# Memory-token attention with a gated MLP, forward and backward: stores on another queue, a normalisation emitted later, eleven head groups

## The chip, the cores and the metric

One core of one Trainium2 chip runs the whole program. The metric is the device time of one execution in microseconds (us); smaller is better. The engines are TensorE (PE in the profile, its weight loads PEld), VectorE (DVE), ScalarE (ACT), GpSimd (POOL) and SyncE (SP, which here only issues DMAs). Each engine works through its own list of instructions in order; semaphores hold an instruction back until what it needs is there, and whatever stands behind it on the same engine waits too.

## The reference

A block with conditioning (six modulation rows from `c`), an attention branch A, a gated MLP branch B, and the gradients of all inputs. What matters is branch A, which is a recurrence:

```python
for s in range(n_seg):                       # 64 segments of 32 rows
    xs = x[:, s * seg_len:(s + 1) * seg_len, :].copy()
    h = jnp.concatenate([mem, xs], axis=1)   # 8 memory rows + 32 rows = 40
    q, k, v = h @ Wq, h @ Wk, h @ Wv         # 32 heads of 128
    p = softmax(where(mask, q k^T * scale, -1e9))
    o = (p v) @ Wo
    mem = o[:, :M, :].copy()                 # the next segment's memory
    outs.append(o[:, M:, :])
```

Segment s cannot start before the first eight output rows of segment s-1 are there. The backward pass runs the same chain from the last segment to the first. (The lines for q, k, v, p and o are shortened.)

## The kernel before

**Phases.** `phase2` is the forward recurrence with the first layer norm in it, `phase3` the MLP forward and backward, `phase4` the backward recurrence, `phase5` the weight gradients of A (large matrix products over rows that phases 2 and 4 left in DRAM). A scheduler orders the instructions of each engine from the program's text and its own estimate of when each becomes ready, so the order on an engine is not that of the source.

**Layout.** 32 heads times 40 rows are kept as groups of three heads: one group holds 3 x 40 = 120 rows in a block of 128 columns. 32 heads need 11 groups (the last holds two). The tiles are built for `G = 12` groups, `G * 128 = 1536` columns, so that three parts (`pi` = 0, 1, 2) of `PG = 4` groups fit the PSUM banks; in phase 2 the twelfth group is skipped by `min(PG, 11 - pi * PG)`, in phase 4 it is computed like the others. Every tile of that layout that goes through DRAM (`OT`, `PS`, `OSR` from phase 2; `DVR`, `DKR`, `DQR` from phase 4) is 128 x 1536 bf16, 384 KB.

**Phase 2, one segment.** `hT` holds the segment's 32 rows: 8 of memory and 24 of x. Its last 8 rows do not depend on the memory; they are projected ahead for four segments at once (`proj_b`, rows `RBv`, `RBk`, `RBq`, turned by `turn_b` into `b_cols`). Position in such a group of four is `s4` (0 to 3); below a *tile* is four segments. For each segment:

- `proj` and `turn` make q, k, v (`RAq`, `RAk`, `RAv`, then `qT`, `kT`, `vT`). The 8 extra columns per head are copied from `b_cols` by GpSimd (L65, four small copies for each of v, k, q).
- The rows of k and q go to DRAM for the backward pass by `rows_out`: two DMAs each on SP (`KST`, `QST`, L455 and L457), and once per tile six DMAs each for the `RB` rows (L461, L464).
- `st_exp` computes the scores and their exponential `ET`, `den` the denominators `rden`, `pv` the output rows `Ost`, `ott` turns them into `OT` (evacuated by ACT, L61), `outproj` multiplies by Wo into `at_ps` (L208).
- `fold_split` cuts `at_ps` into a bf16 head and its remainder (`at_hi` by ACT, L230, `at_lo` by DVE, L231, each in two halves of one tile), `fold_sum` adds the four column blocks (`at_ft`, L239), and ACT copies the memory rows into the next `hT` (L630). That copy ends the segment's part in the recurrence.
- `P` for the backward pass is `ET` transposed by a DMA on SP (`Pst<-ET`, L617; `Pst` has one buffer) and multiplied by `rden` on GpSimd (L635). GpSimd issues the stores of `PS`, `OT`, `OSR` (L637 to L639) and of `VT` (L594).
- `TailRows` collects the last 8 rows of each segment's `OT` on GpSimd (`collect`, L1463, tile `ao_tail`), and after four segments multiplies them by Wo in four pieces (`chunk`, `ao_tps`, L208); their fold goes through `self.later`. `fill(s4, ...)` puts the next tile's `proj_b` and `turn_b` at named places of the segment.

**Phase 4, one segment** (backwards): `OT`, `Pst`, `VT`, `Qst`, `Kst` are loaded on SP; `dot_bank` (`proj_ps`, L1124), `dost`, `ds_part` (L1142, L1146), `grad_part` (L1155) and `dstt` work in parts of four groups; each of dV, dK, dQ is transposed by a DMA on SP (`rows_x`, L1160) and stored by GpSimd (L1161); `dht` sums into `dh_ps`, which is folded as in phase 2 and gives the next segment's `dyT` (L1216).

Of the kernel before, what the change touches and what calls it, by code (L numbers as in the profile page):

```python
# [19 lines left out]
class Cfg:  # L20
    def __init__(self, NS=64, phases=("p0", "p1", "p2", "p3", "p4", "p5")):
        self.S_full = 2048
        self.D = 512
        self.DC = 4
        self.H = 32
        self.E = 128
        self.T = 32
        self.M = 8
        self.L = 40
        self.F = 1792  # L30
        self.FC = 14
        self.NS = NS
        self.S = NS * self.T
        self.NT = self.S // 128
        self.G = 12
        self.XW = 33 * 40 + 8
        self.scale = self.E ** -0.5
        self.phases = phases


class K:
# [181 lines left out]
    def fold_split(self, pool, ps, name):  # L223

        nc = self.nc
        hi = pool.tile([128, 512], BF16, name=name + "_hi", tag="hi")
        lo = pool.tile([128, 512], BF16, name=name + "_lo", tag="lo")
        for h in range(2):
            sl = slice(256 * h, 256 * h + 256)
            nc.scalar.activation(hi[:, sl], ps[:, sl], AF.Copy)  # L230
            nc.vector.tensor_tensor(lo[:, sl], ps[:, sl], hi[:, sl], op=ALU.subtract)  # L231
        return hi, lo

    def fold_sum(self, psp, parts, name, tag):

        ft = psp.tile([128, self.cfg.DC, 32], F32, name=name + "_ft", tag=tag)
        for c in range(self.cfg.DC):
            for i, t in enumerate(parts):
                self.nc.tensor.matmul(ft[:, c, :], lhsT=t[:, c * 128:(c + 1) * 128], rhs=self.foldsel[:],  # L239
                                      start=(i == 0), stop=(i == 1))  # L240
        return ft
# [89 lines left out]
    def phase2(self):  # L331
# [4 lines left out]
        PG = G // NP  # L336
        PW = PG * GW
        with ExitStack() as ctx:
# [74 lines left out]
            def part3(t, pi):  # L413
                return t[:, pi * PW:(pi + 1) * PW].rearrange("p (g x) -> p g x", x=GW)
# [55 lines left out]
            def b_pieces(t):  # L470
# [17 lines left out]
                return {(0, "end1"): [P("k", 0)], (1, "end1"): [P("k", 1)], (2, "end1"): [P("q", 0)], (2, "mid"): [T_("k")],  # L488
                        (2, "end2"): [P("q", 1)], (3, "mid"): [P("v", 0), T_("q")], (3, "end1"): [P("v", 1)], (4, "start"): [T_("v")]}
# [9 lines left out]

            tail = TailRows(self, sb2, psp, psb, 1, "ao", self.AOB)  # L500
            for s in range(NS):
# [24 lines left out]
                def st_exp(pi):  # L526
                    st_ps = ps_f32("st_ps")
                    for j in range(min(PG, 11 - pi * PG)):
# [4 lines left out]
                    n = min(PG, 11 - pi * PG)  # L533
# [4 lines left out]
                def den(pi):  # L538
                    if pi == 0:
                        den_ps[0] = psp.tile([128, G], F32, name="dc_ps", tag="p")  # L540
                    n = min(PG, 11 - pi * PG)
# [6 lines left out]
                def transposes_part(src, pi, w=GW):  # L548
                    ps = ps_b16("tps")
                    n = min(PG, 11 - pi * PG)  # L550
# [9 lines left out]
                def pv(pi):  # L560
                    or_ps = ps_f32("or_ps")
                    n = min(PG, 11 - pi * PG)
# [31 lines left out]
                nc.gpsimd.dma_start(self.VT[s], VT[:, :])  # L594
# [3 lines left out]
                proj("q", 1, "dve")  # L598
                st_exp(0)
# [18 lines left out]
                pv(2)  # L618
                ott(1)
                outproj(0)  # L620
# [6 lines left out]
                self.pop_later()  # L627
# [5 lines left out]
                if s4 == nseg_t - 1:  # L633
                    tail.begin(s - nseg_t + 1, [Wo])
                nc.gpsimd.tensor_tensor(Pst[0:120, 0:11, :], Pst[0:120, 0:11, :],  # L635
                                        rden[:, 0:11].unsqueeze(2).to_broadcast([120, 11, 128]), op=ALU.mult)
                nc.gpsimd.dma_start(self.PS[s], Pst[:])  # L637
                nc.gpsimd.dma_start(self.OT[s], gl3(OT))
                nc.gpsimd.dma_start(self.OSR[s], gl3(Ost))  # L639
# [370 lines left out]
    def phase4(self):  # L1010
# [7 lines left out]
        with self.p4_ctx as ctx:  # L1018
# [10 lines left out]
            PG = G // NP  # L1029
# [24 lines left out]
            def part3(t, pi):  # L1054
                return t[:, pi * PW:(pi + 1) * PW].rearrange("p (g x) -> p g x", x=GW)
# [29 lines left out]
            def transposes_part(src, pi):  # L1085
                ps = ps_b16("tps")
                for j in range(PG):
                    g = pi * PG + j
                    nc.tensor.transpose(ps[:, j, :], src[:, g * GW:(g + 1) * GW], self.ident[:, :])  # L1089
                return ps  # L1090
# [13 lines left out]
            for s in reversed(range(NS)):  # L1104
# [12 lines left out]
                def dot_bank(hb, eng):  # L1117
# [13 lines left out]
                    nc.vector.tensor_tensor(prodO[:, hb * PW:(hb + 1) * PW], dOT[:, hb * PW:(hb + 1) * PW],  # L1131
                                            OT[:, hb * PW:(hb + 1) * PW], op=ALU.mult)

                def dost(pi):
                    ps = transposes_part(dOT, pi)
                    nc.vector.tensor_copy(part3(dOst, pi), ps[:, :, :])

                def ds_part(pi):
                    ps = ps_f32("dp_ps")
                    for j in range(PG):  # L1140
                        g = pi * PG + j
                        nc.tensor.matmul(ps[:, j, :], lhsT=dOT[:, g * GW:(g + 1) * GW], rhs=VT[:, min(g, 10) * 120:min(g, 10) * 120 + GW],  # L1142
                                         start=(j == 0), stop=False, skip_group_check=True)
                    for j in range(PG):
# [3 lines left out]
                    nc.vector.scalar_tensor_tensor(out=part3(dS, pi), in0=ps[:, :, :], scalar=cfg.scale, in1=part3(Pst, pi),  # L1148
                                                   op0=ALU.mult, op1=ALU.mult)

                def grad_part(nm, lh, rh, xt, pi, eng):
                    ps = ps_f32("g_ps")
                    for j in range(PG):
# [3 lines left out]
                    self.evac(eng, part3(xt, pi), ps[:, :, :])  # L1157
# [5 lines left out]
                def dstt(pi):  # L1163
                    ps = transposes_part(dS, pi)
                    nc.vector.tensor_copy(part3(dST, pi), ps[:, :, :])
# [421 lines left out]
```

## Time and profile before

| what | us |
|---|---|
| median of 3 runs | 3884.27 (3883.76 to 3904.68) |
| the profiled execution, its own time | 3890.29 |
| its span from first to last instruction | 3888.5 |
| TensorE busy | 3348.9 (86% of the span) |
| VectorE / ScalarE / GpSimd busy | 1686.8 / 1238.8 / 1102.1 |
| phase 2, first to last `hT` copy | 120.2 to 1391.1 |
| phase 4, first to last `dyT` copy | 2070.6 to 3216.2 |

Busy shares are means over phases with different limits, so each phase is read by itself below. A row of a timeline gives the start, the duration, the engine (SPq is SP's queue), line, operation, out<-in, shapes and count, and in brackets how long the engine had been idle and what released it. A row of waits gives the engine and line that waited, what it waited for, the total, the number of times, and the longest.

### The profile page before, as it was taken

The page shows a single profiled execution, that of the slowest core. Times are in us where ns is not written, and L with a number is a line of the kernel's source. Part 1 is how long each engine was busy: PE and PEld are TensorE (multiplying, and loading weights), DVE is VectorE, ACT ScalarE, POOL GpSimd, SP SyncE. Part 2 cuts the span into 40 slices and gives each one's busy share as a digit, 9 for nine tenths or more (in the row PEclk, how much of TensorE's full clock was granted, in tenths as well). Part 3 has the DMA queues.
Part 4 walks back from the last instruction along what each step waited for, and adds up shares of the span by engine and source line. Part 5 has one row for each costly group of instructions (what it writes and reads, how often), then busy time and mean ns, then how long its engine had stood idle before and what let it go on. Part 6 is the DMA issues. An engine that isn't in the chain of part 4 may idle for free.

```text
span 3888.5 us, 108424 instructions
## 1 busy us (share of the span) xinstructions
PE 3348.9 (86%) x45938; PEld 1940.7 (50%) x46014; DVE 1686.8 (43%) x4087; ACT 1238.8 (32%) x2742; POOL 1102.1 (28%) x2173
## 2 busy tenths in 40 slices
PE   2888888888888869997998989998899994999996
PEld 1444444444444435554545666666566662445453
DVE  2544444444444437764134444544455451322222
ACT  0444444444444435453122322333233331100001
POOL 3444444434433423332112111121112110322221
PEclk6999999999999979999999999999999997999998
DMA  7566655565655663333779999999999999878874
GB/s 227 127 130 134 138 137 130 132 130 137 133 121 125 125 171 121 120 118 106 238 220 232 229 233 219 229 241 224 209 234 244 231 235 194 213 194 200 196 204 144
DMA packets 825642, 692.39 MB, mean 178 GB/s; under 512 B 543850, under 2 KB 716666, under 8 KB 825028
## 3 DMA queue, kind: packets, MB, share of 16 engines
q1 hardware_dynamic: 714852, 422.99, 51.6%
q0 software_dynamic: 51504, 206.62, 15.8%
q10 hardware_dynamic: 58800, 55.84, 5.7%
q8 instruction: 360, 5.90, 0.7%
q14 instruction: 126, 1.03, 0.1%
HBM read 297.01 MB, written 287.61 MB: 150 GB/s over the span
## 4 chain that ended last, share of the span: by engine, by line
PE 55%; DMA 10%; issue 5%; DVE 4%; ACT 2%; POOL 1%; SPq 0%; DVEq 0%; ACTq 0%; POOLq 0%
PE gps L1356 11%; PE dh_ps L208 10%; PE proj_ps L1124 5%; PE g_ps L1155 4%; DMA Pst<-ET 4%; PE gps5o L1366 3%; PE gps L928 3%; PE pass_ps L431 2%; PE mm L842 2%; PE tps L1089 2%; PE dh_tps L208 1%; PE dp_ps L1146 1%; PE dp_ps L1142 1%; PE mm L775 1%; PE mm L779 1%
## 5 line engine op out<-in xcount | busy, mean ns | idle before, releaser
L1356 PE MATMUL gps<-rows,hrows 128*128 128x512 bf16 (+2 forms) x2124 | 415.2, 355 | 1.9
L1356 PEld LDWEIGHTS <-hrows 128*128 128x128 bf16 x2160 | 211.4, 98 | 204.1
L1124 PE MATMUL proj_ps<-dyT,WoT 128*128 128x40 bf16 x8192 | 232.7, 180 | 36.8 <-issue 29.2
L1124 PEld LDWEIGHTS <-WoT 128*128 128x128 bf16 x8192 | 223.3, 96 | 49.8 <-issue 49.8
L635 POOL TENSOR_TENSOR Pst<-Pst,rden 120x1408 bf16<-120x1408 bf16 x64 | 163.2, 2550 | 259.5 <-DMA Pst<-ET 242.1
L431 PEld LDWEIGHTS <-hT 128*32 128x32 bf16 x6144 | 146.4, 99 | 160.9 <-issue 21.0
L63 DVE CAST ot<-gps 128x512 bf16<-128x512 f32 (+3 forms) x77 | 48.9, 635 | 390.9 <-PE gps L1356 206.2
L208 PE MATMUL at_ps<-Wo,OT 128*32 128x512 bf16 x2048 | 169.7, 430 | 49.0 <-ACT OT L61 48.8
L231 DVE TENSOR_TENSOR dh_lo<-dh_ps,dh_hi 128x256 bf16<-128x256 f32 x128 | 54.4, 425 | 333.0 <-ACT dh_hi L230 332.9
L1366 PE MATMUL gps5o<-dyrows,rows 128*128 128x512 bf16 x627 | 139.9, 382 | 45.8 <-DMA rows<-OSR 44.9
L61 ACT ACTIVATE dVT<-g_ps 128x512 bf16<-128x512 f32 x192 | 114.6, 597 | 202.9 <-PE g_ps L1155 156.5
L61 ACT ACTIVATE ot<-gps 128x512 bf16<-128x512 f32 (+3 forms) x77 | 42.5, 552 | 415.4 <-PE gps L1356 239.3
L61 ACT ACTIVATE OT<-tps 128x512 bf16<-128x512 bf16 (+1 forms) x192 | 107.9, 563 | 180.8 <-DMA OT<-OT 79.5
L1360 POOL DMA_DIRECT2D out_dram<-ot x108 | 81.6, 755 | 279.3 <-DVE ot L63 152.0
L63 DVE CAST dKT<-g_ps 128x512 bf16<-128x512 f32 x192 | 131.9, 687 | 63.3 <-PE g_ps L1155 58.8
L208 PE MATMUL dh_ps<-WvT,dVT 128*32 128x512 bf16 x2048 | 153.5, 396 | 3.8 <-issue 3.8
L61 ACT ACTIVATE dOT<-proj_ps 128x480 bf16<-128x480 f32 (+2 forms) x192 | 68.5, 391 | 275.1 <-PE proj_ps L1124 193.5
L231 DVE TENSOR_TENSOR at_lo<-at_ps,at_hi 128x256 bf16<-128x256 f32 x128 | 54.1, 422 | 234.0 <-ACT at_hi L230 231.5
L431 PE MATMUL pass_ps<-Wv,hT 128*32 128x512 bf16 x2048 | 143.1, 422 | 9.5 <-ACT hT L630 9.5
L61 ACT ACTIVATE dQT<-g_ps 128x512 bf16<-128x512 f32 x192 | 114.7, 597 | 112.1 <-PE g_ps L1155 112.1
L63 DVE CAST RAq<-pass_ps 128x512 bf16<-128x512 f32 x128 | 88.5, 692 | 131.4 <-PE pass_ps L431 129.9
L567 DVE TENSOR_TENSOR Ost<-or_ps,rden 120x512 bf16<-120x512 f32 (+1 forms) x192 | 123.6, 644 | 34.4 <-PE dc_ps L544 18.9
(368 smaller groups left out, 7487.5 us busy)
## 6 DMA issues: line engine op xcount, KB each, us to landing
OSR<-Ost POOLq DMA_DIRECT2D x64, 384.0 KB, 4.4
OT<-OT POOLq DMA_DIRECT2D x64, 384.0 KB, 3.3
PS<-Pst POOLq DMA_DIRECT2D x64, 384.0 KB, 4.7
OT_l<-OT SPq DMA_DIRECT2D x64, 384.0 KB
Pst_l<-PS SPq DMA_DIRECT2D x64, 384.0 KB
DVR<-rows_x POOLq DMA_DIRECT2D x64, 384.0 KB, 4.7
DKR<-rows_x POOLq DMA_DIRECT2D x64, 384.0 KB, 6.8
DQR<-rows_x POOLq DMA_DIRECT2D x64, 384.0 KB, 4.3
```

Source lines behind the costliest of these rows:

```text
L61: return nc.scalar.activation(out, in_, AF.Copy)
L63: return nc.vector.tensor_copy(out, in_)
L208: self.nc.tensor.matmul(ps[32 * j:32 * j + 32, :], lhsT=lhsT, rhs=w, start=(n < 4), stop=(n >= total - 4), tile_position=(0, 32 * j))
L231: nc.vector.tensor_tensor(lo[:, sl], ps[:, sl], hi[:, sl], op=ALU.subtract)
L431: nc.tensor.matmul(ps[32 * j:32 * j + 32, :], lhsT=lhs(c), rhs=rhs, start=(c == 0), stop=(c == DC - 1), tile_position=(0, 32 * j))
L567: nc.vector.tensor_tensor(part3(Ost, pi)[0:120, 0:n, :], or_ps[0:120, 0:n, :], rden[:, pi * PG:pi * PG + n].unsqueeze(2).to_broadcast([120 ...
L635: nc.gpsimd.tensor_tensor(Pst[0:120, 0:11, :], Pst[0:120, 0:11, :], rden[:, 0:11].unsqueeze(2).to_broadcast([120, 11, 128]), op=ALU.mult)
L928: nc.tensor.matmul(ps[:], lhsT=h2r[:, j, c * 128:(c + 1) * 128], rhs=xr[:, j, :], start=(j == 0), stop=(j == NT - 1))
L1124: nc.tensor.matmul(ps[:, g_, hl * L:(hl + 1) * L], lhsT=WoT[:, c, h * E:(h + 1) * E], rhs=dyT[:, c, :], start=(c == 0), stop=(c == DC - 1))
L1155: nc.tensor.matmul(ps[:, j, :], lhsT=lh[:, g * GW:(g + 1) * GW], rhs=rh[:, g * GW:(g + 1) * GW], start=True, stop=True)
L1356: nc.tensor.matmul(ps[:, 0:ng * E], lhsT=hrows[:, tp_, c * 128:(c + 1) * 128], rhs=rows[:, tp_, 0:ng * E], start=(tp_ == 0), stop=(tp_ == ...
L1366: nc.tensor.matmul(ps[:], lhsT=rows[:, tp_, gg * E:(gg + 1) * E], rhs=dyrows[:, tp_, :], start=(tp_ == 0), stop=(tp_ == NTP - 1))
```

## The change

Five things change together.

- `G` is 11: all tiles, DRAM tensors, stores, loads and transposes of that layout have 1408 columns (352 KB); in phase 4 the twelfth group is no longer computed. Parts keep four groups (`PG = 4`), the third has three.
- The stores of `VT`, `OT`, `OSR`, `PS` are issued by SP.
- The multiplication of `Pst` by `rden` and the `PS` store are emitted in the next segment, after its `proj`.
- `fold_split` uses four tiles of 256 columns; both `hi` halves come ahead of both `lo` halves.
- In phase 2 the order within a segment and the places of the `proj_b` and `turn_b` pieces differ.

```diff
-        self.G = 12
+        self.G = 11
...
-        hi = pool.tile([128, 512], BF16, name=name + "_hi", tag="hi")
-        lo = pool.tile([128, 512], BF16, name=name + "_lo", tag="lo")
+        parts = []
         for h in range(2):
             sl = slice(256 * h, 256 * h + 256)
-            nc.scalar.activation(hi[:, sl], ps[:, sl], AF.Copy)
-            nc.vector.tensor_tensor(lo[:, sl], ps[:, sl], hi[:, sl], op=ALU.subtract)
-        return hi, lo
+            hi = pool.tile([128, 256], BF16, name=name + "_hi", tag=f"hi{h}")
+            nc.scalar.activation(hi[:], ps[:, sl], AF.Copy)
+            parts.append(hi)
+        for h in range(2):
+            lo = pool.tile([128, 256], BF16, name=name + "_lo", tag=f"lo{h}")
+            nc.vector.tensor_tensor(lo[:], ps[:, 256 * h:256 * h + 256], parts[h][:], op=ALU.subtract)
+            parts.append(lo)
+        return parts
...
-                return {(0, "end1"): [P("k", 0)], (1, "end1"): [P("k", 1)], (2, "end1"): [P("q", 0)], (2, "mid"): [T_("k")],
-                        (2, "end2"): [P("q", 1)], (3, "mid"): [P("v", 0), T_("q")], (3, "end1"): [P("v", 1)], (4, "start"): [T_("v")]}
+                return {(0, "end1"): [P("v", 0)], (1, "end1"): [P("v", 1)], (1, "end2"): [P("k", 0)], (2, "mid"): [T_("v")],
+                        (2, "end1"): [P("k", 1)], (2, "end2"): [P("q", 0)], (3, "end1"): [P("q", 1)], (3, "end2"): [T_("k")],
+                        (4, "start"): [T_("q")]}
...
-                nc.gpsimd.dma_start(self.VT[s], VT[:, :])
+                nc.sync.dma_start(self.VT[s], VT[:, :])
...
+                if norms:
+                    norms.pop()()
                 st_exp(0)
...
                 self.pop_later()
+                vst(2)
                 den(0)
                 pv(0)
-                vst(2)
                 st_exp(1)
                 st_exp(2)
-                ott(0)
+                fill(s4, "mid")
                 den(1)
                 pv(1)
-                tail.chunk()
-                fill(s4, "mid")
+                ott(0)
+                self.pop_later()
                 den(2)
...
                 pv(2)
+                outproj(0)
                 ott(1)
-                outproj(0)
                 ott(2)
...
                 fill(s4, "end1")
-                self.pop_later()
+                tail.chunk()
                 ft = self.fold_sum(psp, parts, "at", "p")
...
-                nc.gpsimd.tensor_tensor(Pst[0:120, 0:11, :], Pst[0:120, 0:11, :],
-                                        rden[:, 0:11].unsqueeze(2).to_broadcast([120, 11, 128]), op=ALU.mult)
-                nc.gpsimd.dma_start(self.PS[s], Pst[:])
-                nc.gpsimd.dma_start(self.OT[s], gl3(OT))
-                nc.gpsimd.dma_start(self.OSR[s], gl3(Ost))
+                nc.sync.dma_start(self.OSR[s], gl3(Ost))
+                nc.sync.dma_start(self.OT[s], gl3(OT))
+
+                def norm(s=s, Pst=Pst, rden=rden):
+                    nc.gpsimd.tensor_tensor(Pst[0:120, :, :], Pst[0:120, :, :],
+                                            rden[:, :].unsqueeze(2).to_broadcast([120, G, 128]), op=ALU.mult)
+                    nc.sync.dma_start(self.PS[s], Pst[:])
+
+                norms.append(norm)
...
             def transposes_part(src, pi):
                 ps = ps_b16("tps")
-                for j in range(PG):
+                n = min(PG, G - pi * PG)
+                for j in range(n):
```

The same replacement of `range(PG)` by `range(n)` is made in `ds_part`, `grad_part` and `dstt` of phase 4.

Where this puts the instructions is seen at three places. The first is TensorE at the end of the last segment of a tile in the middle of phase 2 (`s4 = 3`), before; repeated rows are left out. `at_ft` is the fold that the recurrence waits for, `ao_tail` the collected tail rows of this tile, `p1tp` the first layer norm's transposes for a later tile.

```order
L239 LDWEIGHTS at_hi
L239 MATMUL at_ft<-foldsel,at_hi 128x32
L314 LDWEIGHTS h_14878
L314 MATMUL p1tp<-ident,h_14878 128x128
L208 LDWEIGHTS ao_tail_13656
L208 MATMUL ao_tps<-Wo,ao_tail_13656 32x512
```

With the change the first rows of the same kind stand in the next segment, between its scores (`st_ps`, with the mask) and its second denominators (`dc_ps`).

```order
L538 MATMUL st_ps<-maskT_491,ident 128x120
L208 LDWEIGHTS ao_tail_13727
L208 MATMUL ao_tps<-Wo,ao_tail_13727 32x512
L550 LDWEIGHTS ET_518
L550 MATMUL dc_ps<-ones,ET_518 128x1
L571 LDWEIGHTS ET_518
L571 MATMUL or_ps<-Vst_520,ET_518 128x128
```

Nine of the tail's matmuls thus stood ahead of the last three of the fold that ends the segment; now the first of them comes behind most of the next segment's scores.

The second place is GpSimd around the multiplication of `Pst` at that tile boundary, before.

```order
L65 COPY qT_512<-b_colsq 128x24x8
L635 TENSOR_TENSOR Pst<-Pst,rden 120x1408
L639 DMA OSR<-Ost_522 128x1536
L1463 COPY ao_tail_13656<-OT_524 128x33x8
L637 DMA PS<-Pst 128x1536
L638 DMA OT<-OT_524 128x1536
L318 COPY hb<-hx 128x128
```

And with the change:

```order
L647 TENSOR_TENSOR Pst<-Pst,rden 120x1408
L1479 COPY ao_tail_13727<-OT_524 128x33x8
L65 COPY kT_514<-b_colsk 128x3x8
L322 COPY hb<-hx 128x128
L65 COPY kT_514<-b_colsk 128x24x8
L65 COPY kT_514<-b_colsk 128x3x8
L65 COPY kT_514<-b_colsk 128x2x8
L65 COPY qT_512<-b_colsq 128x3x8
L65 COPY qT_512<-b_colsq 128x24x8
```

The multiplication still stands ahead of the collection of its own segment's tail rows. The three stores are gone from this engine, and at this boundary the k and q copies of the next segment stand behind the multiplication; at the other three boundaries of a tile they stand ahead of it, before and with the change.

The third place is SP between two transposes, before (`H1ROWS` once per tile).

```order
L617 DMA_TRANSPOSE Pst<-ET_518 128x12x128
L311 DMA H1ROWS<-h_18022 128x512
L455 DMA KST<-RAk_528 3x32x1024
L457 DMA KST<-RAk_528 32x3x384
L455 DMA QST<-RAq_530 3x32x1024
L457 DMA QST<-RAq_530 32x3x384
```

And with the change, at the same boundary:

```order
L625 DMA_TRANSPOSE Pst<-ET_518 128x11x128
L643 DMA OSR<-Ost_522 128x1408
L644 DMA OT<-OT_524 128x1408
L649 DMA PS<-Pst 128x1408
L465 DMA QST<-RBq_536 4x8x1024 x3
L468 DMA QST<-RBq_536 4x8x384 x2
L315 DMA H1ROWS<-h_18117 128x512
L600 DMA VT<-vT_516 128x1328
L459 DMA KST<-RAk_528 3x32x1024
L461 DMA KST<-RAk_528 32x3x384
L459 DMA QST<-RAq_530 3x32x1024
L461 DMA QST<-RAq_530 32x3x384
```

`OSR` and `OT` follow the transpose directly; the `PS` store, which waits for the multiplication, stands ahead of the `RB` rows and of the next segment's `VT`, `KST` and `QST`.

More of the change, by code (lines that the diff above doesn't have):

```diff
@@ L527, in st_exp @@
                     st_ps = ps_f32("st_ps")
-                    for j in range(min(PG, 11 - pi * PG)):
+                    for j in range(min(PG, G - pi * PG)):
                         g = pi * PG + j
@@ L1152, in grad_part @@
                     ps = ps_f32("g_ps")
-                    for j in range(PG):
+                    n = min(PG, G - pi * PG)
+                    for j in range(n):
                         g = pi * PG + j
```

45 lines of the change are left out of this document (24 added, 21 removed).

## The prediction

> **What bounds the kernel now.** I read the page's slices first, then the ends of the segments and the stretches of the two recurrences, then the waits of TensorE in each, and last the timeline around the longest waits.
>
> ```profile
> PE   2888888888888869997998989998899994999996
> L630 ACT ACTIVATE hT<-at_ft x63: 197/198/198, 120.2 to 1391.1; 128x32 bf16<-128x32 f32 x63
> L1216 ACT ACTIVATE dyT<-dh_ft x63: 197/198/198, 2070.6 to 3216.2; 128x32 bf16<-128x32 f32 x63
> 120.00:1391.00 1271.00, 1083.16 (x16515) 583.10 (x16513) 583.88 (x1751) 556.37 (x1433) 512.22 (x1257) 0.94 0.59 131
> 2070.00:3216.00 1146.00, 1056.94 (x21206) 715.35 (x21205) 567.74 (x1297) 356.13 (x772) 217.33 (x448) 0.97 1.03 230
> ```
>
> TensorE is the busiest engine everywhere, but the phases differ in what interrupts it. The copy that ends a segment runs 63 times in 1270.9 us in phase 2, 20.5 us a segment (62 intervals), and in 1145.6 us in phase 4, 18.5 us. The last two numbers of the stretches are the DMA share and GB/s: transfers are at 0.59 in phase 2 and at 1.03 in phase 4. The change touches only these two phases, so I price them apart.
>
> **Phase 2: the waits that the change aims at.** The waits of TensorE there, one of ScalarE below them:
>
> ```profile
> PE ao_tps L208 <- POOL ao_tail L1463: 69.8, 15, 8.5
> PE at_ps L208 <- ACT OT L61: 43.7, 14, 4.9
> PE tps L553 <- ACT OT L61: 12.2, 4, 4.4
> ACT at_hi L230 <- DVE at_lo L231: 26.3, 62, 0.5
> ```
>
> The first comes 15 times, once per tile. Its place is the end of an `s4 = 3` segment:
>
> ```profile
> 821.29 4.00 SPq L617 DMA_TRANSPOSE Pst<-ET  x1
> 829.01 2.53 POOL L635 TENSOR_TENSOR Pst<-Pst,rden 120x1408 bf16<-120x1408 bf16 x1 [8.88 <-DMA Pst<-ET]
> 832.07 0.42 POOL L1463 COPY ao_tail<-OT 128x264 bf16<-128x264 bf16 x1
> 832.54 1.46 PE L208 MATMUL ao_tps<-Wo,ao_tail 128*32 128x512 bf16 x9 [8.53 <-POOL ao_tail L1463]
> 834.23 0.20 ACT L630 ACTIVATE hT<-at_ft 128x32 bf16<-128x32 f32 x1 [9.59 <-PE at_ft L239]
> ```
>
> The transpose takes 7.7 us from issue to the start of the multiplication; GpSimd stands at that multiplication, the tail's collection stands behind it, and TensorE stands at the tail's matmuls with the rest of the segment's own fold behind them. In the changed order those matmuls come behind most of the next segment's scores, whose first exponential starts 7.6 us into a segment further down (945.74 less the end of the copy, 938.16); the collection still stands behind the multiplication, but that much earlier than it is needed. I take all **69.8 us**.
>
> The second and third have one cause, seen in an `s4 = 2` segment:
>
> ```profile
> 877.94 2.54 POOL L635 TENSOR_TENSOR Pst<-Pst,rden 120x1408 bf16<-120x1408 bf16 x1 [1.50 <-DMA Pst<-ET]
> 880.42 0.58 POOL L638 DMA_DIRECT2D OT<-OT  x1
> 881.53 0.54 POOL L594 DMA_DIRECT2D VT<-vT  x1
> 886.32 0.60 ACT L61 ACTIVATE OT<-tps 128x512 bf16<-128x512 bf16 x1 [5.47 <-DMA OT<-OT]
> ```
>
> The last segment's `OT` store is issued behind the multiplication, lands late, and ScalarE may not overwrite `OT`. With the change SP issues it right behind the transpose, ahead of anything that waits for the multiplication. What cover it has is seen in a segment without long waits:
>
> ```profile
> 937.96 0.20 ACT L630 ACTIVATE hT<-at_ft 128x32 bf16<-128x32 f32 x1 [0.30 <-PE at_ft L239]
> 945.74 0.57 ACT L534 ACTIVATE ET<-st_ps 128x480 bf16<-128x480 f32 x1 [0.60 <-ACT qT L61]
> 948.85 0.60 ACT L61 ACTIVATE OT<-tps 128x512 bf16<-128x512 bf16 x1 [0.28 <-issue]
> 954.04 0.76 POOL L65 COPY kT<-b_colsk 128x192 bf16<-128x192 bf16 x4
> ```
>
> (The last row, copies for the next segment, is used further down.) `OT` is rewritten 10.7 us after the copy that began the segment; the transpose before it had landed by the multiplication at 941.15 (its row is below), 3.0 us into it. That leaves 7.7 us for a store of 352 KB whose predecessor took 5.9 (880.42 to 886.32). I take 43.7 + 12.2 = **55.9 us**.
>
> Separate halves in the fold remove ScalarE's wait for the first `at_lo`, 26.3 us in 62 times. TensorE has the `proj_b` matmuls to do in some of that time; bounds 0 and 26, I take half, **13 us**. Together 139 us, and the remaining TensorE time of a tile is 4 x 20.5 - 139/16 = 73.3 us.
>
> **Phase 2: what comes in its place.** SP now carries a chain through every segment: multiplication, `PS` store, `VT` store, k and q rows, transpose, next multiplication. Its pieces, from two segments before:
>
> ```profile
> 901.12 0.71 SPq L455 DMA_DIRECT2D KST<-RAk  x1
> 905.18 3.23 SPq L617 DMA_TRANSPOSE Pst<-ET  x1
> 912.47 2.86 POOL L635 TENSOR_TENSOR Pst<-Pst,rden 120x1408 bf16<-120x1408 bf16 x1 [4.39 <-DVE ao_b_tb L247]
> ...
> 927.32 0.72 SPq L455 DMA_DIRECT2D KST<-RAk  x1
> 931.41 4.23 SPq L617 DMA_TRANSPOSE Pst<-ET  x1
> 941.15 2.54 POOL L635 TENSOR_TENSOR Pst<-Pst,rden 120x1408 bf16<-120x1408 bf16 x1 [5.49 <-DMA Pst<-ET]
> ...
> 872.82 2.42 SPq L461 DMA_DIRECT2D KST<-RBk  x3
> 875.28 1.21 SPq L464 DMA_DIRECT2D KST<-RBk  x2
> ```
>
> From the first k row store to the multiplication are 11.4 us and 13.8 us. The multiplication adds 2.54, the issues of `PS` and `VT` 0.54 each (the row of `VT` above): 15.0 to 17.4 us for a plain segment, under TensorE's 73.3 / 4 = 18.3. In two of four segments five or six `RB` stores now stand between `PS` and `VT`: five cost 2.42 + 1.21 = 3.6 us, six about 4.3. The four segments of a tile then make 4 x 15.0 + 0.6 + 4.3 + 3.6 = 68.5 us at the lower length and 78.1 at the upper, against 73.3. The lower adds nothing; the upper adds 4.8 us a tile, 77 us in all. Both are near; I take 2.3 us a tile, **37 us**. The trace cannot show this chain on one queue, so both ends stay in the range. GpSimd loses four issues of about 0.55 us a segment, which it had spare.
>
> [...]
>
> **Phase 4.** Per segment eight movements of a 384 KB tile (two loads, three transposes, three stores) shrink by 32 KB each.
>
> ```profile
> DMA packets 396215, 263.95 MB, mean 230 GB/s; under 512 B 344328, under 2 KB 344328, under 8 KB 396012
> q1 hardware_dynamic: 378697, 185.25, 81.2%
> q0 software_dynamic: 17315, 75.67, 20.4%
> q8 instruction: 166, 2.72, 1.0%
> PE proj_ps L1124 <- issue: 29.2, 10, 5.7
> PE g_ps L1155 <- issue: 13.5, 9, 2.6
> PE tps L1089 <- issue: 11.1, 6, 3.9
> ACT dh_hi L230 <- DVE dh_lo L231: 30.2, 62, 0.5
> 2504.29 0.39 PE L1142 MATMUL dp_ps<-VT_l,dOT 128*128 128x128 bf16 x4
> 2505.64 0.39 PE L1155 MATMUL g_ps<-dS,Qst 128*128 128x128 bf16 x4
> ```
>
> The two queues fill the engines (81.2% + 20.4%), yet TensorE hardly waits for data: its long waits are for "issue", 53.8 us in these three rows, in the middle of a run of equal matmuls. The profile names no releaser; 166 transfers of queue q8, each 16 KB of instructions, cross the same engines, and I read the waits as instructions that come late behind data. So the phase is paced by transfers, indirectly. Eight times 32 KB is 0.262 MB of 4.26 MB a segment (263.95 / 62); at 230 GB/s that is 1.14 us, 73 us over 64 segments. From TensorE's side: seven transposes and matmuls a segment go (one each in `dost` and `dstt`, two in `ds_part`, three in `grad_part`). Six groups of four start within 1.35 us between the two last rows, 0.056 us each, so 0.39 us a segment and 25 us in all; the fold's wait is worth up to 30, half of it 15. That is 40 us if transfers pace nothing, and 40 + 54 = 94 if the issue waits go as well. I take **70 us**, near the transfer number.
>
> [...]
>
> **The sum.** 69.8 + 55.9 + 13 - 37 + 70 = 172 us off the profiled 3890.29 gives 3718; the median of the runs lies 6.0 us under that execution, so **3712 us**.
>
> **Rivals.**
> - *SP's chain paces phase 2.* At 78.1 us a tile phase 2 gains 139 - 77 = 62 and the total is 132: 3752 us. For it: TensorE's margin over the plain chain is 1 to 3 us. Against: the k rows are ready early in a segment, so the chain can run ahead. Chance 0.2.
> - *The change does not move the multiplication.* In GpSimd's order it still stands right behind the transpose's wait and, at a tile's boundary, now ahead of the next k and q copies, which the first scores need. If those 15 waits of 69.8 us come back at the scores, 102 us are left: 3782 us. For it: the order. Against: the first scores end 7.6 us into a segment, the multiplication started 3.0 us into that one, and it, the collection and two sets of four copies make 2.5 + 0.4 + 2 x 0.76 = 4.5 us, just in time. Chance 0.12.
> - [...] Chance 0.06.
> - *Phase 4 is not paced by transfers*: 142 us, 3742 us. Chance 0.13.
> - *Both phases fall to TensorE's own time*: no new wait in phase 2, 94 in phase 4, 233 us: 3651 us. Chance 0.1.
> - *Slower.* With `PS`, `VT`, `OSR` and `OT` on its queue the transpose lands later in every segment. Chain per segment: k row store to multiplication, plus 3.6 us, plus 2.1 us for the `RB` stores as a mean of four. It passes 20.5 us, today's segment, at 14.8 us, and eats phase 4's 70 us (1.1 a segment) at 15.9. At 18 us a segment would take 23.7, phase 2 would lose 205 us, and the total would be 3884 + 205 - 70 = 4019. For it: 13.8 is close to 15.9. Against: that 13.8 already holds the same stores, which ran beside it on the other queue. Chance 0.06.
>
> The forecast itself, within 30 us, has 0.33. The range reaches from **3640** (just under the case of TensorE's own time) to **3815**, over the rivals that end faster; what lies beyond is the slower case, and sums of two rivals. About 1% is what a measurement of this kernel can tell from no change, 39 us: faster **0.89**, same **0.05**, slower **0.06**, since only two or more rivals together end within 1%.
>
> **What the changed profile would show.** The wait of `ao_tps` for the collection and the wait of `OT`'s evacuation for its store are gone from phase 2; ScalarE's second `hi` no longer waits for the first `lo`. The interval of the `hT` copy falls from 20.5 to about 18.9 us, that of `dyT` from 18.5 to about 17.4. If SP's chain paces, the multiplication waits for the transpose in every segment and TensorE waits for `kT` or `qT` copies of GpSimd or for `ET`. Phase 4's DMA share stays near 1 with a shorter interval if transfers pace it, and falls with an unchanged interval if they don't. The prediction is wrong if the transpose takes over 12 us from issue in most segments, or if the scheduler's new order makes TensorE stand at something that is late on another engine, as it did at the tail.

## The result and the profile after

The changed kernel takes 3696.07 us (3693.98 to 3704.61), 0.949 of the time before, 3894.47 us in the runs beside it (95% interval 0.945 to 0.953). The forecast was 3712. The profiled execution took 3698.06 us with a span of 3696.3, 192.2 less than before.

TensorE's slices on the page after, in tenths, from 8 to 9 in the second half of phase 2 (slices 9 to 14):

```profile
PE   1889888899999969996989999999999994999996
```

The copies that end a segment, in both recurrences:

```profile
L638 ACT ACTIVATE hT<-at_ft x63: 192/197/197, 120.1 to 1282.3; 128x32 bf16<-128x32 f32 x63
...
L1232 ACT ACTIVATE dyT<-dh_ft x63: 197/197/198, 1953.7 to 3029.1; 128x32 bf16<-128x32 f32 x63
```

The two stretches (length; busy time of PE, PEld, DVE, ACT and POOL; granted clock, DMA share, GB/s):

```profile
120.00:1282.00 1162.00, 1056.06 (x16512) 581.09 (x16509) 577.36 (x1748) 546.36 (x1431) 380.62 (x1025) 0.97 0.62 136
1954.00:3029.00 1075.00, 1017.89 (x20767) 677.52 (x20766) 530.46 (x1296) 337.04 (x771) 215.27 (x447) 0.98 1.08 230
```

A segment of phase 2 takes 18.75 us instead of 20.50: 108.7 us in all. One of phase 4 takes 17.34 instead of 18.48: 70.1 us. The other 13 us lie outside the two recurrences (8 between them, 5 behind the second).

TensorE's waits in phase 2 after (total, times, longest):

```profile
PE turn_ps L442 <- DVE RAq L63: 38.0, 7, 5.8
PE at_ps L208 <- ACT OT L61: 24.3, 50, 0.8
PE st_ps L536 <- POOL qT L65: 10.4, 11, 3.0
PE pass_ps L435 <- ACT hT L638: 9.1, 18, 0.6
PE ao_tps L208 <- POOL ao_tail L1479: 8.2, 1, 8.2
```

`ao_tps` has gone from 69.8 us to 8.2, `OT` from 43.7 + 12.2 in 18 waits of up to 4.9 to 24.3 in 50, none over 0.8. Two rows are new: `RAq`, 38.0 us in 7, and `qT`, 10.4. The copies show where the first sits: with few exceptions three of a tile's four segments take 17.1 to 17.3 us, but the first takes 26.3 to 27.8 in seven tiles (segments 8 to 32) and, but for one of 23.0, 18 to 20 us later. The timeline in one of them, which begins at the copy at 724.43 and ends at 751.30:

```profile
728.71 2.53 POOL L647 TENSOR_TENSOR Pst<-Pst,rden 120x1408 bf16<-120x1408 bf16 x1 [8.37 <-DMA Pst<-ET]
731.26 0.32 SPq L649 DMA_DIRECT2D PS<-Pst  x1
731.68 1.96 SPq L465 DMA_DIRECT2D QST<-RBq  x3
733.68 1.21 SPq L468 DMA_DIRECT2D QST<-RBq  x2
735.48 0.37 SPq L300 DMA_DIRECT2D x<-in_A_x_dram  x1
737.60 0.69 DVE L302 BATCH_NORM_STATS2 st<-x 128x6 f32<-128x512 bf16 x1 [6.97 <-DMA x<-in_A_x_dram]
738.62 0.68 DVE L63 CAST RAq<-pass_ps 128x512 bf16<-128x512 f32 x1
739.36 0.61 PE L442 MATMUL turn_ps<-ident,RAq 128*128 128x128 bf16 x4 [5.32 <-DVE RAq L63]
```

The layer norm's load of `x` for a later tile stands on SP behind the `PS` store, which waits for the multiplication, which waits for the transpose. VectorE stands at that `x`; the evacuation of `RAq`, which the recurrence needs, stands behind it. Of the sixteen `x` loads eight are issued before the first `hT` copy. From 264 us on one falls into each of the seven long segments, and VectorE waits 6.4 to 8.0 us for it; the last is the one above, which is why the long segments end there.

The clock lies in the same segment. Here are the segment ahead of it, the long one, 6.8 us out of its middle, and the segment behind it (columns as above):

```profile
707.30:724.43 17.13, 15.79 (x258) 8.96 (x255) 8.75 (x27) 9.86 (x26) 4.48 (x8) 1.00 0.67 140
724.43:751.30 26.87, 20.51 (x289) 11.44 (x289) 12.10 (x36) 9.07 (x24) 11.09 (x28) 0.87 0.52 153
738.30:745.10 6.80, 5.74 (x60) 4.49 (x61) 4.27 (x14) 1.76 (x5) 3.08 (x14) 0.50 0.40 86
751.30:768.49 17.19, 16.62 (x266) 8.89 (x262) 8.78 (x27) 7.78 (x21) 3.62 (x15) 1.00 0.59 83
```

TensorE waits 5.3 us for `RAq`, until 739.36, and the clock is halved from 738.3 to 745.1; the 5.7 us that TensorE is busy there lose 2.9 us of work. Together that is 8.2 us, and by 8.2 this segment exceeds the 18.7 us of a first segment without the wait (below, with `PS` on GpSimd). The segment behind it has the full clock and takes 17.19 us. By the trace's records of the granted clock all seven long segments have 6.8 us at half clock, beginning 3.4 to 4.6 us into a wait of TensorE of 5.3 to 5.8 us.

Phase 4 after, TensorE's waits:

```profile
PE proj_ps L1138 <- issue: 11.8, 8, 2.8
PE g_ps L1171 <- DMA Kst<-KST: 9.5, 7, 2.5
PE dp_ps L1157 <- issue: 5.8, 3, 2.5
PE dh_ps L208 <- issue: 4.5, 4, 2.5
```

All of TensorE's waits for issue there, the smaller rows included, fell from 66 to 31 us; the sums below are made the same way, so they are a little above those that some expectations quote.

### The profile page after: what moved, and what is told of

Same layout as the page of the kernel before. It is cut to its first block, busy times and chain, and to the rows that moved or that the text cites. A ratio compares the mean times of both kernels' runs of the same rounds, so it can differ in the third digit from the quotient of the medians.

```text
span 3696.3 us, 108208 instructions
## 1 busy us (share of the span) xinstructions
PE 3282.3 (89%) x45566; PEld 1897.6 (51%) x45566; DVE 1640.8 (44%) x4087; ACT 1208.9 (33%) x2742; POOL 957.9 (26%) x1917
## 4 chain that ended last, share of the span: by engine, by line
PE 53%; DMA 5%; issue 3%; DVE 3%; ACT 1%; SPq 1%; POOL 0%; DVEq 0%; ACTq 0%; POOLq 0%
PE gps L1372 11%; PE dh_ps L208 10%; PE proj_ps L1138 6%; PE g_ps L1171 4%; PE gps5o L1382 3%; PE gps L941 3%; PE mm L855 3%; PE dh_tps L208 2%; PE tps L1103 2%; DMA Kst<-KST 2%; PE mm L788 1%; PE mm L792 1%; PE dp_ps L1161 1%; PE dp_ps L1157 1%; PE pass_ps L435 1%
## 5 line engine op out<-in xcount | busy, mean ns | idle before, releaser
L1138 PE MATMUL proj_ps<-dyT,WoT 128*128 128x40 bf16 x8192 | 233.1, 180 | 19.4 <-issue 11.8
L208 PE MATMUL at_ps<-Wo,OT 128*32 128x512 bf16 x2048 | 135.0, 384 | 27.9 <-ACT OT L61 25.4
L61 ACT ACTIVATE dVT<-g_ps 128x512 bf16<-128x512 f32 (+1 forms) x192 | 107.8, 561 | 157.3 <-PE g_ps L1171 119.2
L61 ACT ACTIVATE dQT<-g_ps 128x512 bf16<-128x512 f32 (+1 forms) x192 | 107.8, 561 | 125.1 <-PE g_ps L1171 125.1
L63 DVE CAST dKT<-g_ps 128x512 bf16<-128x512 f32 (+1 forms) x192 | 123.7, 644 | 44.0 <-PE g_ps L1171 43.2
L208 PE MATMUL dh_ps<-WkT,dKT 128*32 128x512 bf16 x2048 | 136.7, 388 | 0.0
L435 PE MATMUL pass_ps<-Wv,hT 128*32 128x512 bf16 x2048 | 126.8, 391 | 9.4 <-ACT hT L638 9.4
```

The source lines that it names most:

```text
L61: return nc.scalar.activation(out, in_, AF.Copy)
L63: return nc.vector.tensor_copy(out, in_)
L208: self.nc.tensor.matmul(ps[32 * j:32 * j + 32, :], lhsT=lhsT, rhs=w, start=(n < 4), stop=(n >= total - 4), tile_position=(0, 32 * j))
L435: nc.tensor.matmul(ps[32 * j:32 * j + 32, :], lhsT=lhs(c), rhs=rhs, start=(c == 0), stop=(c == DC - 1), tile_position=(0, 32 * j))
L1138: nc.tensor.matmul(ps[:, g_, hl * L:(hl + 1) * L], lhsT=WoT[:, c, h * E:(h + 1) * E], rhs=dyT[:, c, :], start=(c == 0), stop=(c == DC - 1))
```

## The experiments

Intervals are from the first to the last copy over 62. Ratios are to the kernel before, run beside each.

| kernel | us | ratio, 95% | `hT` interval | `dyT` interval |
|---|---|---|---|---|
| changed | 3696.07 | 0.949 [0.945, 0.953] | 18.75 | 17.34 |
| changed, once more | 3683.32 | 0.944 [0.940, 0.948] | 18.62 | 17.20 |
| x load on ScalarE | 3655.22 | 0.939 [0.937, 0.942] | 18.14 | 17.58 |
| four stores on GpSimd | 3698.73 | 0.952 [0.949, 0.954] | 18.77 | 17.16 |
| tail chunk earlier | 3758.22 | 0.966 [0.963, 0.968] | 19.70 | 17.24 |
| before with G = 11 | 3834.75 | 0.987 [0.984, 0.990] | 20.50 | 17.62 |
| x one tile early | 3679.81 | 0.944 [0.939, 0.948] | 18.56 | 17.36 |
| 12 groups of bytes | 3767.08 | 0.966 [0.960, 0.972] | 18.74 | 18.36 |
| two stores left out | 3669.01 | 0.941 [0.937, 0.946] | 18.64 | 16.84 |
| fold as before | 3745.16 | 0.960 [0.955, 0.965] | 19.22 | 17.28 |
| **PS on GpSimd** | **3626.98** | 0.930 [0.926, 0.935] | 17.67 | 17.24 |
| two transposes left out | 3635.91 | 0.933 [0.928, 0.937] | 18.70 | 16.32 |
| the same as PS, transposes in pieces | 3660.11 | 0.939 [0.934, 0.944] | 17.62 | 18.10 |

**How far one program varies.**

> The changed kernel itself once more, to see how far its phase 4 and its issue waits vary between executions and to have its time beside the two others on the same chip: 3696 us (3690 to 3706); a dyT interval of 17.2 to 17.6 us and issue waits of 25 to 45 us would put the differences of phase 4 among kernels with the same phase 4 down to that; an interval of 17.34 within 0.05 would make them effects of the kernels.

3683.32 us, interval 17.20, issue waits 30 us. All kernels here with the changed phase 4 lie between 17.16 and 17.58, with issue waits of 30 to 49 us, so differences under 0.4 us a segment there, and issue waits within that span, are not read.

**One part seems to be no change at all.** With the multiplication emitted in its own segment again, every row on every engine comes out in the same order, so "one segment late" decides nothing; I take it that the scheduler ranks by readiness. This is read from the order of instructions alone, and no run shows it. The trace before fits: there the multiplication already ran 3.0 us into the next segment (941.15 against 938.16).

**What removed the tail's wait.**

```diff
                 ott(0)
+                tail.chunk()
                 self.pop_later()
...
                 fill(s4, "end1")
-                tail.chunk()
```

> The changed kernel with one line moved back: tail.chunk() is called in the middle of a segment, behind ott(0), not behind the end1 pieces. In TensorE's order the first ao_tps matmuls then stand again ahead of the last fold matmuls of the tile's last segment. Theory: this place alone made the 69.8 us wait of ao_tps for the collection, so it comes back: 3696 + 70 = 3766 us (3745 to 3790). Rival: the queues or the late multiplication removed the wait, and the place does nothing: 3696 us within 15, with no ao_tps wait of over 20 us.

```profile
PE ao_tps L208 <- POOL ao_tail L1479: 114.1, 15, 8.9
```

The wait is back 15 times, and the time rises by 62 to 75 us over the two series of the changed kernel. The first segment of a tile falls from 23.6 to 19.6 us at the same time (such means are over segments 5 to 56): I read it as the x load having time to arrive during the wait of 7 to 9 us at the end of a tile. So the place of `chunk` removed the wait.

**What the queue did.**

```diff
-                nc.sync.dma_start(self.VT[s], VT[:, :])
+                nc.gpsimd.dma_start(self.VT[s], VT[:, :])
...
```
(and likewise `OSR`, `OT`, `PS`)

> The changed kernel with the four stores VT, OSR, OT and PS of phase 2 issued by GpSimd again; the order on TensorE, ScalarE and VectorE is the same row by row. Theory: the queue is what removed the wait of OT's evacuation for its own store (43.7 + 12.2 us before), so it comes back: +56 us; but the x load no longer stands behind PS, so the eight long segments go: -66 us. Together 3686 us (3670 to 3705), with both waits seen to change places. Rival: TensorE's and ScalarE's new order removed the OT wait, not the queue: the OT wait stays away, only the -66 remain, 3630 us.

```profile
PE at_ps L208 <- ACT OT L61: 55.0, 49, 6.0
PE st_ps L536 <- POOL qT L65: 10.9, 11, 1.9
```

Both mechanisms show: `OT` rises from 24.3 to 55.0 us and the third segments from 17.2 to 21.2, while the `RAq` row goes and the first segments fall from 23.6 to 19.6. They cancel: moving all four stores is worth nothing, 3698.73 against 3696.07 and 3683.32.

**The new wait.** Two attempts on the x load, then one on what it stands behind.

```diff
-            nc.sync.dma_start(x0[:], x_rows[j * 128:(j + 1) * 128, :])
+            nc.scalar.dma_start(x0[:], x_rows[j * 128:(j + 1) * 128, :])
```

> The changed kernel with one edit: the layer norm's load of x (x0 in p1_tile) is issued by ScalarE instead of SyncE. Theory: in eight of the sixteen tiles the first segment of a tile takes 26 to 28 us instead of 18 to 19, because this load stands on SyncE's queue behind the PS store, which waits for the multiplication and so for the transpose; VectorE stands at the load and TensorE at VectorE's evacuation of RAq. Those eight segments should fall to 18 to 19 us, TensorE's wait turn_ps <- DVE RAq (39.9 us in 8) should be gone, and the granted clock of the segment behind (0.81) should be near 1. Time 3696 - 8 x 8.2 = 3630 us (3620 to 3645). Rival: the order of VectorE's work makes the segment long, whatever queue the load is on: time stays at 3696 us within 10.

3655.22 us: part of it. The clock of 0.81 in this expectation belongs, by the segments' own bounds shown above, to the long segments themselves. ScalarE now stands, in a row that has nothing to do with the transpose:

```profile
681.88 0.60 ACT L61 ACTIVATE RAv<-pass_ps 128x512 bf16<-128x512 f32 x1 [1.21 <-PE pass_ps L435]
686.48 0.33 ACTq L300 DMA_DIRECT2D x<-in_A_x_dram  x1
686.86 0.60 ACT L61 ACTIVATE b_colsq<-turn_ps 128x512 bf16<-128x512 bf16 x1 [4.38 <-DMA Pst<-ET]
```

The program's own order explains it. The semaphores of SP's and ScalarE's DMAs are eight counters used in turn (`DMAHW0` to `DMAHW7` in this listing; in the trace of the changed kernel 2077 of 2172 of these DMAs carry the semaphore of the one issued eight before), so each issue below also waits for the DMA eight before it in the program:

```
L459 DMA KST<-RAk_528 3x32x1024 [waits DMAHW6_49,Activation_49]
L461 DMA KST<-RAk_528 32x3x384 [waits DMAHW7_49]
L459 DMA QST<-RAq_530 3x32x1024 [waits DMAHW0_49,DVE_49]
L461 DMA QST<-RAq_530 32x3x384 [waits DMAHW1_49]
```

For this x load the trace names the transpose, 4.38 us: both carry the same semaphore. First segments fell to a mean of 20.8 us, not to 18 to 19 (23.6 before the edit; long ones had been seven, not eight).

```diff
+        def x_load(j):                 # two buffers; p1_tile(j) ends with x_load(j + 1)
+            xs[j] = p1w.tile([128, D], BF16, name="x0_1", bufs=2)
+            nc.sync.dma_start(xs[j][:], x_rows[j * 128:(j + 1) * 128, :])
```

> The changed kernel with the layer norm's load of x one tile early (two buffers, still on SyncE's queue), so that nothing waits for it. Theory: with the load on ScalarE the wait only moved, because that load itself waited for the transpose (ScalarE's 4.38 us ahead of b_colsq) and held back the evacuation of RAk; with the load 70 us early both waits go, the first segments of the tiles take 18.6 us instead of 23.6, and the time is 3630 us (3618 to 3642). Rival: what holds the tile's first segment is the mass of transfers there (x, RB rows and PS together), not the load's place: some other row is late, and the time stays near ScalarE's variant, 3655 us.

```profile
482.02 0.32 SPq L657 DMA_DIRECT2D PS<-Pst  x1
486.62 0.88 SPq L303 DMA_DIRECT2D x<-in_A_x_dram  x1
489.20 0.69 DVE L309 BATCH_NORM_STATS2 st<-x 128x6 f32<-128x512 bf16 x1 [5.13 <-DMA x<-in_A_x_dram]
```

The edit missed its aim: the reader moved forward with the load, the two stand 2.6 us apart again, and six long segments stayed.

```diff
-                    nc.sync.dma_start(self.PS[s], Pst[:])
+                    nc.gpsimd.dma_start(self.PS[s], Pst[:])
```

> The changed kernel with the PS store alone back on GpSimd, where the multiplication that it waits for runs; VT, OSR and OT stay on SyncE, and the order on TensorE, ScalarE and VectorE is the same row by row. Theory: SyncE's queue then holds nothing that waits for the multiplication, so x and the RB rows are issued in time and the first segments of the tiles fall from 23.6 to about 19.4 us as with all four stores on GpSimd, while OT's store stays early and the OT wait stays near 25 us: 3696 - 64 = 3632 us (3618 to 3645). Rival: what makes x late is the number of stores on SyncE's queue (each issue there waits for the one eight before it), not the PS store's wait: the long segments stay at 23 us or more, time 3680 us or over.

```profile
PE at_ps L208 <- ACT OT L61: 24.5, 51, 0.6
...
PE turn_ps L442 <- DVE RAq L63: 2.7, 7, 0.5
```

Its stretch of phase 2:

```profile
119.00:1214.00 1095.00, 1037.37 (x16509) 566.28 (x16509) 590.08 (x1748) 545.78 (x1430) 420.21 (x1086) 0.99 0.67 145
```

3626.98 us, 56 below the changed kernel beside it, and faster than both kernels: the intervals 0.926 to 0.935 and 0.940 to 0.948 do not meet. First segments take 18.7 us. `OT` keeps its early store; the `RAq` wait falls from 38.0 to 2.7 us, the `qT` row is gone, and VectorE no longer waits for `x` by more than 0.1 us in phase 2. One store with a late operand ahead of the x load was the cause; the other three stores are still on this queue.

**The fold.**

```diff
-        return parts                    # four tiles of 256 columns
+        return hi, lo                   # two tiles of 512, half by half
```

> The changed kernel with the fold as before: hi and lo in one tile each, written half by half in turn. Theory: ScalarE's second hi waits for the first lo again, 0.4 us a fold, and it costs TensorE 0.28 us a segment in both phases: 18 us each, time 3696 + 36 = 3732 us (3718 to 3745). Rival: in phase 2 the proj_b matmuls hide it, so only phase 4 pays: 3714 us; or neither, 3696 us.

49 to 62 us slower. Phase 2 alone gives 29.4 us in the profile against the changed kernel's first profile and 37.3 against its second; two of a tile's three plain segments go from 17.2 to 17.9 us, the third stays at 17.1. Phase 4 at 17.28 is inside the spread. So the `proj_b` matmuls do not hide it in phase 2. The profiled execution, at 3732.55 us, was the fastest of four and 34 to 55 us slower than the two profiled ones of the changed kernel; the rest of the difference is not placed.

**Phase 4: arithmetic or bytes.**

```diff
-        self.G = 12
+        self.G = 11
```
(in the kernel before, with the slices that this needs)

> The kernel before with one part of the change: G = 11 everywhere, and nothing else (fold, queues and order as before). Theory: phase 4 is paced by transfers, 0.262 MB less per segment at 230 GB/s is 1.14 us: the dyT interval falls from 18.5 to 17.4 us and the time from 3894 by 73 to 80 us to about 3818 (3805 to 3830), phase 2 unchanged at 20.5 us a segment. Rival: phase 4 is paced by TensorE, which loses 0.39 us a segment: interval 18.1, time 3894 - 25 = 3869 us.

56 us, 0.86 us a segment, with phase 2 at the same 20.50. Between the two; the next run separates them.

```diff
-        self.G = 11                     # widths of tiles and transfers
+        self.G = 12
-                n = min(PG, G - pi * PG)   # matmuls, transposes, copies
+                n = min(PG, 11 - pi * PG)
```

> The changed kernel with the matrices OT, P, OSR and the gradient rows 12 groups wide again in memory and in every transfer, but TensorE, ScalarE and VectorE working on 11 groups as in the changed kernel. It tells bytes from arithmetic in phase 4. Theory (transfers pace): the dyT interval rises from 17.3 by 0.5 to 0.9 us, the waits of TensorE for issue rise from 27 towards 46 us, time 3696 + 45 = 3741 us (3725 to 3755). Rival (TensorE's own rows pace): the interval stays at 17.3 us, time 3700 us.

```profile
PE g_ps L1171 <- DMA Kst<-KST: 40.5, 20, 4.5
PE proj_ps L1138 <- issue: 16.2, 8, 4.8
```

18.36 us a segment: the bytes alone return 1.0 of the 1.14 us, though less as waits for issue (42 us in all, inside the span above) than as `Kst` arriving late. The bytes carry the gain of phase 4; whether those of the loads, the stores or the transposes, this run does not tell. In phase 2, at 18.74, they cost nothing.

**Phase 4: what holds back the instructions.**

```diff
+                        if nm == "dVT":
                             nc.gpsimd.dma_start(self.DVR[s], rows[:])
```

> The changed kernel without two of the three stores of gradient rows in phase 4 (those of dK and dQ; phase 5 reads the rows of dV in their place, so out_3 and out_4 are not the gradients). That takes 0.70 MB of about 4 MB from each segment and nothing from TensorE. Theory (transfers pace phase 4, by instructions that come late): the issue waits of TensorE fall from 27 us to under 8, the dyT interval from 17.3 to TensorE's own 16.4 to 16.6 us, time 3696 - 52 = 3644 us (3632 to 3656). Rival: the issue waits have another cause and stay, interval 17.3, time 3696 us.

16.84 us a segment, waits for issue 25 us, not under 8: these stores do not cause most of them. The engines stay nearly full without them, a DMA share of 0.95 (the last column but one):

```profile
1955.00:2999.00 1044.00, 1003.26 (x20771) 670.48 (x20770) 529.39 (x1296) 337.52 (x772) 150.52 (x324) 1.00 0.95 194
```

Then the two transposes as well:

```diff
                         if nm == "dVT":
+                            rows = rxp.tile([128, G, 128], BF16, name="rows_x")
+                            nc.sync.dma_start(rows[:], xt[:, :], transpose=True)
                             nc.gpsimd.dma_start(self.DVR[s], rows[:])
```

> The changed kernel without the transposes of dK and dQ in phase 4 and without their stores (phase 5 reads the rows of dV in their place, so out_3 and out_4 are not the gradients). Against the run without the stores alone, in which TensorE still waited 22 us for issue and the dyT interval was 16.8 us, it takes away two of three transposes. Theory (transposes hold back the fetch of instructions): the issue waits fall under 8 us, the interval to 16.3 to 16.5, time 3696 - 55 = 3641 us (3630 to 3652). Rival (the fetches are late whatever data moves): issue waits of 15 us or more stay, interval 16.7 to 16.9, time 3665 us.

TensorE's one row of waits for issue:

```profile
PE proj_ps L1138 <- issue: 0.5, 1, 0.5
```

and the stretch of phase 4:

```profile
1952.00:2963.00 1011.00, 996.95 (x20762) 668.16 (x20759) 525.50 (x1296) 337.48 (x771) 150.22 (x324) 1.00 0.65 156
```

One wait of 0.5 us is left, and the segment is TensorE's own 16.32 us. That these waits are fetches of instructions shows in the transfers, here around the longest of the kernel before, first in the timeline:

```profile
2392.69 0.33 PE L1124 MATMUL proj_ps<-dyT,WoT 128*128 128x40 bf16 x5 [5.73 <-issue]
```

and the queues from 2388 to 2392.7 (packets, MB, share of 16 engines):

```profile
q1 hardware_dynamic: 510, 0.39, 64.9%
q0 software_dynamic: 41, 0.20, 19.4%
q8 instruction: 1, 0.02, 3.4%
```

In the packet records, 25 of the 26 waits for issue of over 1 us in phase 4 before, and all 12 after, end 1.1 to 1.8 us behind the end of a 16 KB packet of q8; moments so far behind such a packet are 10 to 11% of the phase. The 25 packets before start 10.2 us (median) behind the previous one, the other packets of q8 6.1 us. In the ten us ahead of the 25, transposing packets take 0.78 of the 16 engines' time and all else 0.36; ahead of the others it is 0.47 and 0.55. So the late fetches follow stretches full of transposes. One rival stays open: two transposes fewer also bring the DMA share from 0.95 to 0.65, so no run separates transposing as such from the engine time that it takes. With three whole transposes a segment the waits for issue come to 66 us before, 31 after and 25 without two of the stores; with one transpose, to 0.5.

```diff
+                    if pi == 1:          # groups 0 to 7; the last three at pi == 2
+                        nc.sync.dma_start(rows_x[nm][:, 0:8, :], xt[:, 0:8 * GW], transpose=True)
```

> The faster version (PS store on GpSimd) with each of phase 4's three transposes in two pieces, eight groups as soon as they are there and three at the end; the stores are unchanged. Theory: a fetch of instructions waits behind one whole transpose, and two or three stand together in each segment, so shorter and earlier pieces let it through sooner: issue waits 29 to about 15 us, dyT interval 17.2 to 17.0, time 3627 - 15 = 3612 us (3602 to 3622). Rival: it is the sum of transposed bytes that fills the path, or SyncE's three more issues a segment cost as much: issue waits of 25 us or more, time 3622 to 3650 us.

```profile
PE g_ps L1171 <- DMA Kst<-KST: 55.2, 30, 3.7
PE proj_ps L1138 <- issue: 8.5, 7, 3.1
```

The waits for issue fell from 31 to 17 us, near the theory's 15, but the time rose by 33. SP spends 633 us issuing transposes instead of 448, the `Kst` load behind them is issued 3.5 us into a segment instead of 1.1 (medians), and TensorE waits for it instead.

## Why the prediction was right, and where not

The forecast gain was 172 us and the profiled one 192. The terms were further off than the sum, so that the total came so near is in part luck.

- **Tail, 69.8 us: right.** 61.6 gone, by the place of `chunk`, as worked out from the order. The rival that the wait returns at the scores was true for 10.4 us (`qT`). Its premise, that the multiplication does not move, holds in the order of instructions; but the `qT` row is gone with `PS` on GpSimd, where the multiplication stands in the same place.
- **OT, 55.9 us: mechanism right, size off.** 31.6 gone, and with the stores on GpSimd 30.7 come back, in waits of up to 6.0 us. The 24.3 left are 50 waits of half a microsecond, and stay with `PS` on GpSimd too (24.5), so they are not the store's; I read them as the evacuation itself, 0.56 us, now close to its readers. The term did not ask what would be late next there.
- **Fold, 13 us in phase 2: too small,** 29 to 37. The guess that the `proj_b` matmuls hide half of it failed; the 15 us of phase 4 are inside the spread there.
- **SP's chain, -37 us: wrong place, and too small.** The new waits are 38.0 + 10.4 us, with 6.8 us at half clock at each of the seven for `RAq`; with `PS` alone off SP phase 2 gains 59 to 67 us (18.62 or 18.75 to 17.67 a segment). The step priced the chain by its length against a segment. GpSimd does wait for the transpose 347 us in all, but plain segments run at 17.2 us regardless. The cost came from one row that I had not followed past the `PS` store, the x load: the prediction counted `VT`, rows and `RB` stores behind it and never asked who reads through that queue.
- **That moving the stores gives nothing** was given 0.06. Net it was true for all four stores: two waits changed places. Three of the four, without `PS`, are worth about 72 (3698.73 to 3626.98, from two series).
- **Phase 4, 70 us: right,** 70.1, carried by the bytes. That it fits to 0.1 us is luck: with the spread of 17.16 to 17.58 the gain is 56 to 82. The three rows of "issue" that the prediction added up, 53.8 us, were not all: it is 66. The reading of "issue" as late fetches was right (25 of the 26 long ones end 1.1 to 1.8 us behind a packet of q8), "behind data" only in part: behind transposes, hardly behind plain stores (25 of 31 us stay without two stores, 0.5 without the two transposes as well).
- **Not in the sum: the clock.** TensorE's busy time in phase 2 fell from 1083 to 1056 us with nothing taken away there. Busy time times clock is 1018 before, 1024 after, 1027 with `PS` on GpSimd (0.94, 0.97, 0.99): the work is the same within 1%. TensorE was busy at half clock for 116 us of phase 2 before, 54 after and 9.5 with `PS` on GpSimd, and with each of TensorE's waits of over 4 us there, 22 before and 8 after, came half clock. I put the 27 us down to these waits being fewer.
- **Not in the sum: other waits of phase 2.** TensorE's waits for `ET` at the denominators fell from 19.4 to 8.1 us, and those for `Ost` at the turns, 10.1 us, are gone. I take these for the new order within the segment, which no run tests by itself. These, the clock and the 13 us outside the recurrences (not traced further) made up for the terms that fell short.

## What to carry to other kernels

Where a queue issues in order, as SP's does here (the x load at 735.48 us behind the `PS` store at 731.26), ask of each DMA not how long it takes but what it waits for, and who reads what stands behind it: put a store whose operand is late on the engine that produces the operand (`PS`, 56 us here). Before crediting a program-order edit, compare the instruction order it produces; here one part of the change seems to leave it as it was. When a phase is full of transfers and TensorE waits for issue, look at which kind of transfer these waits go with (here 25 us of them without two stores, 0.5 without two transposes as well), and price a long TensorE wait with the half clock that came with it here, 6.8 us at each of the seven waits of 5.3 to 5.8 us.

## What the runs showed of the hardware

With a wait of TensorE of 5.3 us came 6.8 us at half the granted clock, 1.1 us of them still inside the wait; 2.9 us of work were lost, all in the same segment. In phase 4 TensorE waited up to 5.7 us for instructions, mostly behind stretches full of transposing DMAs (0.78 of the 16 engines' time in the ten us ahead of 25 late packets of instructions in the kernel before, against 0.47 ahead of the others): leaving out plain stores of 0.70 MB a segment left 25 us of these waits of 31, leaving out the transposes of the same rows as well left 0.5.
